# Spectral filter and feed-forward block: loads of x issued earlier in a period, and one first-stage piece of batch three one step sooner

## The chip, the cores and the metric

The kernel runs on one core of a Trainium2 chip. The metric is device time in microseconds; lower is better. A core has five engines that run side by side: TensorE (PE) multiplies matrices, VectorE (DVE) and ScalarE (ACT) work on elements, GpSimd (POOL) here only issues transfers, and SyncE (SP) only issues transfers too. Sixteen DMA engines move the data. Transfers issued by POOL run in one queue (q0) and those issued by SP in another (q1).

## The reference, cut to what matters

```python
# x: (8, 3008, 256), filters: (1505, 256)
X = np.fft.rfft(x, axis=1)
y = np.fft.irfft(X * (filt_r + 1j * filt_i)[None], n=3008, axis=1)
h = y.reshape(24064, 256) @ w_in            # (24064, 2048)
g = np.maximum(h, 0) + alpha * np.minimum(h, 0)
out = g @ w_out                             # (24064, 256)
```

## The kernel before, in words

**Two streams of work in one order.** The feed-forward part works on `yT`, the filtered sequence with the 256 features on partitions, in 48 blocks of 512 tokens (384 in blocks 5, 17, 29 and 41). A block has 16 steps, one for each 128 columns of `w_in`, so the program has 768 steps and block n begins at step 16n. In each step `up` (L473) issues two matmuls (L478) into a PSUM buffer `hps`; after every second step ScalarE evicts the pair to `gtb` (L486) and VectorE applies the slope (L489, L490). The second product, with `w_out`, is spread over the steps of the block after. Most blocks do it directly (`eight`, L515); the blocks of `FAST` do it with seven products in place of eight (`seven`, L537), for which sums of quarters of `gtb` are formed ahead (`sums`, L492): two on VectorE (L498, L500) and four as accumulating transfers that POOL issues, two of L502 (gtb<-gtb) and two of L504 (gtb<-ss). The table `SUMS` puts the latter at the steps 13, 17, 19 and 22 counted from the block's begin. The last of the seven products, sixteen matmuls, reads what L504 wrote: the first eight read the first transfer's half, the last eight the second's.

The filter is a Fourier transform done as matmuls, batch by batch, in stages that are put between these steps by hand. The function `put(step, fn)` files an action under a step, and the loop at the end calls, step by step, what is filed there and then `up`. An engine's queue, and SP's and POOL's queues of transfers, run in that order. For batch index b (0 to 7; batch three is b = 2) the stages are:

- **Load** (`load_x`, L145): the batch comes in four chunks `xs`, each in two transfers that POOL issues (L148), converting to 16 bits. There are four such buffers, so the chunks of a batch take the buffers of the batch before.
- **First stage** (`piece_a`, L182): 16 pieces, four to a chunk. One matmul (L190) into a PSUM bank `psF`, evicted by ScalarE to `asb` (L260). After each chunk `save_a` (L194, transfer at L195) writes `asb` to DRAM. There are two `asb` buffers, so chunk 3 (pieces 12 to 15) takes the buffer of chunk 1 (pieces 4 to 7).
- **Turn** (`turn_a`, L202): SP reads it back from DRAM into `at`, turned.
- **Second stage** (`piece_b`): 12 pieces, two matmuls each (L210), multiplied with the filter by VectorE into `ww` and `uu` (L213, L214), and joined by two accumulating transfers of POOL (L216, uu<-ww).
- **Third stage** (`piece_c`): two matmuls (L228), evicted to `v`. After every third piece `turn_c` (L231) writes part of `v` to DRAM in four transfers of SP (L237). After the last one three loads `zt` (L246) read it back; each waits until all writes have landed. The fourth `zt` load comes later.
- **Fourth stage** (`piece_d`): 16 pieces of four matmuls (L253) on `zt`, evicted to `yT`, where the feed-forward part reads.

All stage matmuls but some of the first batch's go through two `psF` banks, whose order is written out by hand in `BANKS`.

**Where the change lies.** For batches one and two (b = 1, 2) the steps come from `plan_fft` (L598). For b = 2 it has a0 = 66 and ga = 2, so piece i stands at step 66 + 2i: piece 7 at 80, and the save of its chunk at 80 too, after the second batch's last `turn_c` with its three `zt` loads, which is filed under step 80 first. Piece 12 stands at step 90, and the second batch's fourth stage begins at step 92. For b from 3 to 7 the steps count from p = 96(b − 1), the begin of a period of six blocks (p = 192, 288, 384, 480, 576), by the tables `STEPS_A` to `STEPS_D` (L29 to L32); its loads of the next batch are filed under p + 6, 10, 16 and 20 (L643), with b up to 6. The next batch's first pieces, which read these loads, stand at p + 15 and later. In a period the second stage stands at −19, −16, −16, −3, 1, 10 and later, the third at −5, 7, 8, 16, 20 and later. A block of `FAST` begins at each p, and another 32 steps ahead of p; the L504 transfers of that one are filed under p − 13 and p − 10.

Of the kernel before, what the change touches and what calls it, by code (L numbers as in the profile page):

```python
# [10 lines left out]
FP16 = mybir.dt.float16  # L11
# [6 lines left out]
D = 256  # L18
# [62 lines left out]
def kernel(  # L81
# [10 lines left out]
    nc = tc.nc  # L92
# [12 lines left out]
    p_as = ctx.enter_context(tc.tile_pool(name="p_as", bufs=2))  # L105
# [9 lines left out]
    a_dram = dram.tile([NB, 96, NH, D], FP16, name="a_dram")  # L115
# [25 lines left out]
    def xrow(b, h, c):  # L141
        return bass.AP(tensor=x.tensor, offset=x.offset + (b * NFFT + NH * h + 8 * c) * D,
                       ap=[[N2 * D, N1], [1, 8 * D]])

    def load_x(b, c):  # L145
        xs = p_x.tile([2 * N1, 8 * D], FP16, name="xs")
        for h in range(2):
            nc.gpsimd.dma_start(out=xs[h * N1 : h * N1 + N1], in_=xrow(b, h, c))  # L148
        return xs
# [14 lines left out]
    def bank(wide=False):  # L164
        if wide:
            return psH.tile([128, 2, 512], FP32, name="hps")[:, 0]
        return psF[int(next(order))].tile([128, 512], FP32, name="psF")
# [8 lines left out]
    class Fft:  # L176
        def __init__(self, b):
            self.b = b
            self.base = (b % 2) * NFFT
            self.uw, self.zt = {}, {}  # L180

        def piece_a(self, i, evict, wide=False):  # L182
            if i == 0:
                self.at = p_fft.tile([128, NK1, D], FP16, name="at")
            if i % 4 == 0:
                self.asb = p_as.tile([96, 8, D], FP16, name="asb")
            xs = xc[(self.b, i // 4)]
            ps = bank(wide)
            o = (i % 4) * 512
            nc.tensor.matmul(ps[0:96], wf1_s, xs[:, o : o + 512], start=True, stop=True)  # L190
            u = 2 * (i % 4)
            evict(self.asb[:, u : u + 2].rearrange("p a d -> p (a d)"), ps[0:96])

        def save_a(self, c):  # L194
            nc.sync.dma_start(out=a_dram[self.b, :, 8 * c : 8 * c + 8], in_=self.asb)  # L195

        def turn_a(self, eng, ka=0, kb=NK1):
            for h in range(2):
# [138 lines left out]
    xc = {(0, c): load_x(0, c) for c in range(4)}  # L337
# [76 lines left out]
    for q in range(2):  # L414
        nc.gpsimd.dma_start(
            out=wout_s[:, 8 * q : 8 * q + 8],
            in_=moe_w_out[1024 * q : 1024 * q + 1024].rearrange("(j p) d -> p j d", p=128))
# [177 lines left out]
    def put(step, fn, *args):  # L595
        plan.setdefault(step, []).append((fn, args))

    def plan_fft(b, a0, ga, ta, b0, gap, add, lag, d0, quarters, x_at):  # L598
        f = Fft(b)
        for i in range(16):  # L600
            put(int(a0 + ga * i), f.piece_a, i, on_act)
        for c in range(4):
            put(int(a0 + ga * (4 * c + 3)), f.save_a, c)
            if b + 1 < NB:
                put(x_at[c],
                    lambda b=b, c=c: xc.update({(b + 1, c): load_x(b + 1, c)}))
        for q in range(quarters):
            w = NK1 // quarters
            put(ta, f.turn_a, nc.sync, w * q, w * q + w)
        bs = [b0 + (2 * int(gap * kp / 2) if add else int(gap * kp)) for kp in range(12)]  # L610
        for kp in range(12):
            put(bs[kp], f.piece_b, kp)
            put(bs[kp] + lag, f.piece_c, kp, on_act)
        for q in range(4):
            put(bs[3 * q + 2] + lag + 1, f.turn_c, q)
        for i in range(16):
            put(d0 + min(i, 4) + 2 * max(i - 4, 0), f.piece_d, i, on_act)
        put(d0 + 5, f.load_z, 3)
# [9 lines left out]
    for i in range(4):  # L628
        put(26 + 3 * i, neg, 6 * i, 6 * i + 6)
    plan_fft(1, 16, 1, 32, 40, 3, 0, 6, 92, 4, (20, 24, 74, 75))  # L630
    plan_fft(2, 66, 2, 97, 109, 4.5, 8, 12, 187, 4, (110, 114, 118, 122))
    for b in range(3, NB):
        p = 96 * (b - 1)
        f = Fft(b)
        steps_a = STEPS_A if b > 3 else [int(2.4 * i) - 68 for i in range(16)]
        steps_b = STEPS_B if b > 3 else [max(st, 2 * kp - 12) for kp, st in enumerate(STEPS_B)]
        for i in range(16):
            put(p + steps_a[i], f.piece_a, i, on_act)
            if i % 4 == 3:
                put(p + steps_a[i] + 1, f.save_a, i // 4)  # L640
        if b + 1 < NB:
            for c in range(4):
                put(p + (6, 10, 16, 20)[c], lambda b=b, c=c: xc.update({(b + 1, c): load_x(b + 1, c)}))  # L643
        put(p + steps_a[15] + 4, f.turn_a, nc.sync)
        for kp in range(12):
            put(p + steps_b[kp], f.piece_b, kp)
            put(p + STEPS_C[kp], f.piece_c, kp, on_act)
            if kp % 3 == 2:
                put(p + STEPS_C[kp] + 1, f.turn_c, kp // 3)
        for i in range(16):  # L650
            put(p + STEPS_D[i], f.piece_d, i, on_act)
        put(p + STEPS_D[3] + 2, f.load_z, 3)
# [76 lines left out]
```

## Time and profile before

| what | value |
|---|---|
| median of three runs | 798.35 us (797.43 to 800.0) |
| the profiled execution | 798.93 us |
| its span, from the first to the last instruction | 797.1 us |
| granted TensorE clock, mean | 0.998 |
| instructions | 18089 |
| ScalarE busy / VectorE busy | 604.4 us / 685.0 us |
| transfers of POOL's queue (q0) | 50.09 MB, 38.6% of 16 DMA engines |
| transfers of SP's queue (q1) | 69.52 MB, 32.7% of 16 DMA engines |
| L148 loads of xs, 64 transfers, issue to landing | 6.6 us median |
| L502 and L504, 38 each, issue to landing | 4.5 and 6.4 us median |

The profile's page gives shares over the whole span. The waits view lists who waited for whom (total, number, longest). The timeline gives the instructions in order of time, merged where the same operation repeats; a bracket at the end is the engine's idle time before it and what ended it. Times count from the span's begin. Block 0 begins at 37.4 us, block 5 (step 80) at 125.0, block 11 (step 176) at 225.0, block 12 (step 192) at 243.0, block 30 (step 480) at 524.1.

### The profile page before, as it was taken

The numbers are of one execution on the slowest core, as the hardware profiler recorded it, in microseconds if no ns is written. First come the engines' busy times: TensorE is split into PE (matmuls) and PEld (weight loads), VectorE is DVE, ScalarE is ACT, GpSimd is POOL, SyncE is SP. The second block draws the span as 40 slices with busy tenths as digits, with TensorE's granted clock in tenths as the row PEclk, the third lists the DMA queues.
The fourth block names the chain that finished last, engine by engine and source line by source line (L and its number), as shares of the span: only waits on it lengthen the run. The fifth ranks groups of instructions, "written<-read, shape, count | busy, mean of one in ns | idle before, by whom it ended". The sixth has DMA issues, their size and how long they took to land.

```text
span 797.1 us, 18089 instructions
## 1 busy us (share of the span) xinstructions
PE 765.7 (96%) x6856; PEld 540.2 (68%) x6856; DVE 685.0 (86%) x1489; ACT 604.4 (76%) x896; POOL 266.5 (33%) x353
## 2 busy tenths in 40 slices
PE   7899998999999999999999999999999999999998
PEld 6756655666666766766667767667666777767766
DVE  3788984689778898999989999899998999979994
ACT  4688676877768887788868878688877777787763
POOL 7720441063223342452415422434423324102210
PEclk9999999999999999999999999999999999999999
DMA  9995557586596768986797956978688556645642
GB/s 191 186 210 159 110 123 197 142 146 138 119 204 123 151 148 179 205 161 144 168 194 157 189 136 153 237 144 164 142 182 199 108 97 121 154 86 104 129 95 67
DMA packets 113807, 120.84 MB, mean 152 GB/s; under 512 B 12648, under 2 KB 94328, under 8 KB 113592
## 3 DMA queue, kind: packets, MB, share of 16 engines
q0 software_dynamic: 33584, 50.09, 38.6%
q1 hardware_dynamic: 79992, 69.52, 32.7%
q8 instruction: 54, 0.88, 0.5%
q14 instruction: 33, 0.27, 0.1%
q10 hardware_dynamic: 144, 0.07, 0.0%
HBM read 56.06 MB, written 46.66 MB: 129 GB/s over the span
## 4 chain that ended last, share of the span: by engine, by line
PE 65%; DMA 13%; DVE 11%; ACT 6%; issue 3%; SPq 1%; POOL 1%; DVEq 0%; ACTq 0%; POOLq 0%
PE hps L478 28%; PE op L515 17%; PE op L537 9%; DVE m L489 4%; DMA gtb<-ss 4%; ACT gtb L486 3%; DMA at<-a_dram 3%; PE psF L190 3%; DVE gtb L490 3%; PE psF L228 2%; PE psF L253 2%; PE psF L210 2%; DMA uu<-ww 2%; DVE ww L213 1%; DVE uu L214 1%
## 5 line engine op out<-in xcount | busy, mean ns | idle before, releaser
L486 ACT ACTIVATE gtb<-hps 128x1024 f16<-128x1024 f32 (+1 forms) x384 | 385.7, 1005 | 109.9 <-PE hps L478 105.4
L478 PE MATMUL hps<-yT,win_s 128*128 128x512 f16 (+1 forms) x1536 | 450.0, 375 | 0.4 <-ACT gtb L486 0.2
L489 DVE TENSOR_SCALAR m<-gtb,alm_s 128x512 f16<-128x512 f16 (+1 forms) x768 | 235.6, 349 | 68.5 <-ACT gtb L486 65.9
L490 DVE TENSOR_TENSOR gtb<-gtb,m 128x1024 f16<-128x1024 f16 (+1 forms) x384 | 261.6, 681 | 18.4
L515 PE MATMUL op<-wout_s,gtb 128*128 128x256 f16 x1728 | 262.8, 273 | 0.0
L216 POOL DMA_DIRECT2D uu<-ww x168 | 140.2, 986 | 330.3 <-DVE uu L214 157.1
L515 PEld LDWEIGHTS <-gtb 128*128 128x128 f16 x1728 | 168.6, 98 | 114.1 <-issue 0.5
L478 PEld LDWEIGHTS <-win_s 128*128 128x128 f16 x1536 | 137.7, 98 | 32.1 <-issue 8.4
L537 PEld LDWEIGHTS <-gtb 128*128 128x128 f16 x1520 | 103.5, 97 | 49.2 <-DMA gtb<-ss 1.6
L502 POOL DMA_DIRECT2D gtb<-gtb x38 | 42.8, 1127 | 137.0 <-PE hps L478 43.5
L260 ACT ACTIVATE asb<-psF 96x512 f16<-96x512 f32 x112 | 66.1, 594 | 20.4 <-PE psF L190 16.8
L537 PE MATMUL op<-wout_s,gtb 128*128 128x128 f16 x912 | 77.5, 219 | 1.5 <-DMA gtb<-ss 0.8
L260 ACT ACTIVATE yT<-psF 128x376 f16<-128x376 f32 x120 | 56.7, 489 | 8.8 <-PE psF L253 7.7
L260 ACT ACTIVATE v<-psF 128x512 f16<-128x512 f32 x84 | 49.7, 598 | 16.4 <-PE psF L228 15.2
L213 DVE TENSOR_TENSOR ww<-psF,filts_s 128x512 f16<-128x512 f32 x84 | 57.4, 684 | 0.6 <-PE psF L210 0.6
L214 DVE TENSOR_TENSOR uu<-psF,filt_s 128x512 f16<-128x512 f32 x84 | 57.2, 681 | 0.0
L537 PEld LDWEIGHTS <-ss 128*128 128x128 f16 x608 | 42.6, 97 | 21.0
L537 PE MATMUL op<-tw_s,gtb 128*128 128x128 f16 x608 | 52.6, 219 | 0.0
L537 PE MATMUL op<-tw_s,ss 128*128 128x128 f16 x608 | 52.5, 219 | 0.0
L148 POOL DMA_DIRECT2D xs<-in_x_dram x64 | 44.3, 942 | 19.9 <-PE psF L190 13.0
L190 PE MATMUL psF<-xs,wf_s 94*96 94x512 f16 x112 | 42.2, 383 | 5.6 <-ACT asb L260 3.4
L504 POOL DMA_DIRECT2D gtb<-ss x38 | 41.5, 1236 | 6.6 <-PE hps L478 2.6
(85 smaller groups left out, 506.0 us busy)
## 6 DMA issues: line engine op xcount, KB each, us to landing
out_dram<-osb SPq DMA_DIRECT2D x127, 128.0 KB
xs<-in_x_dram POOLq DMA_DIRECT2D x64, 188.0 KB, 6.6
a_dram<-asb SPq DMA_DIRECT2D x28, 384.0 KB
uu<-ww POOLq DMA_DIRECT2D x168, 64.0 KB, 3.1
v_dram<-v SPq DMA_DIRECT2D x112, 96.0 KB
zt<-v_dram SPq DMA_DIRECT2D x28, 384.0 KB
gtb<-gtb POOLq DMA_DIRECT2D x38, 256.0 KB, 4.5
gtb<-ss POOLq DMA_DIRECT2D x38, 256.0 KB, 6.4
```

The costliest lines, as they stand in the source:

```text
L148: nc.gpsimd.dma_start(out=xs[h * N1 : h * N1 + N1], in_=xrow(b, h, c))
L190: nc.tensor.matmul(ps[0:96], wf1_s, xs[:, o : o + 512], start=True, stop=True)
L213: nc.vector.tensor_mul(ww, px, filts_s[:, 2 * kp : 2 * kp + 2])
L214: nc.vector.tensor_mul(uu, px, filt_s[:, 2 * kp : 2 * kp + 2])
L216: nc.gpsimd.dma_start(out=uu[o : o + 64], in_=ww[64 - o : 128 - o], accum_op=OP.add)
L260: nc.scalar.activation(o, i, AF.Copy)
L478: nc.tensor.matmul(self.hps[:, j % 2, 0:tn], win_s[:, kt, j * 128 : (j + 1) * 128], yT[:, kt, self.t0 : self.t0 + tn], start=(kt == 0), st ...
L486: nc.scalar.activation(g, hs, AF.Copy)
L489: nc.vector.tensor_scalar(ms[:, i], g[:, i], 0.0, a, OP.min, OP.mult)
L490: nc.vector.tensor_add(g, g, ms)
L515: nc.tensor.matmul(op[:, si % 2], self.pair(k // 2)[:, k % 2, 128 * si : 128 * si + 128], wout_s[:, k], start=(k == 0), stop=(k == 15))
L537: nc.tensor.matmul(acc[:, 128 * i : 128 * i + 128], x[:, k, 128 * i : 128 * i + 128], b[:, k], start=first and k + i == 0, stop=k == 7, sk ...
```

## The change

One: for b = 3 to 6 the loads of the next batch's four chunks are filed under p − 8, p − 4, p and p + 4 in place of p + 6, p + 10, p + 16 and p + 20. Two: for b = 2, piece 7 and the save of its chunk are filed under step 79 in place of 80. Three: the `asb` buffers are kept by chunk, in a dictionary, in place of one name for the latest.

```diff
         def __init__(self, b):
             self.b = b
             self.base = (b % 2) * NFFT
-            self.uw, self.zt = {}, {}
+            self.uw, self.zt, self.asb = {}, {}, {}
...
             if i % 4 == 0:
-                self.asb = p_as.tile([96, 8, D], FP16, name="asb")
+                self.asb[i // 4] = p_as.tile([96, 8, D], FP16, name="asb")
...
-            evict(self.asb[:, u : u + 2].rearrange("p a d -> p (a d)"), ps[0:96])
+            evict(self.asb[i // 4][:, u : u + 2].rearrange("p a d -> p (a d)"), ps[0:96])
...
-            nc.sync.dma_start(out=a_dram[self.b, :, 8 * c : 8 * c + 8], in_=self.asb)
+            nc.sync.dma_start(out=a_dram[self.b, :, 8 * c : 8 * c + 8], in_=self.asb[c])
...
         for i in range(16):
-            put(int(a0 + ga * i), f.piece_a, i, on_act)
+            put(int(a0 + ga * i) - (b == 2 and i == 7), f.piece_a, i, on_act)
         for c in range(4):
-            put(int(a0 + ga * (4 * c + 3)), f.save_a, c)
+            put(int(a0 + ga * (4 * c + 3)) - (b == 2 and c == 1), f.save_a, c)
...
             for c in range(4):
-                put(p + (6, 10, 16, 20)[c], lambda b=b, c=c: xc.update({(b + 1, c): load_x(b + 1, c)}))
+                put(p - 8 + 4 * c, lambda b=b, c=c: xc.update({(b + 1, c): load_x(b + 1, c)}))
```

The instruction lists show what moves. VectorE's order is the same. On TensorE one L190 moves ahead of the two L478 and four L515 of step 79. On ScalarE one eviction to `asb` moves ahead of one eviction to `gtb`. On SP one save (L195) moves ahead of four v writes (L237) and three zt loads (L246). On POOL, in the periods with p = 288, 384 and 480, the order L504 twice, L216 four times, L148 four times, L216 twice, L502, L148 twice, L502, L504, L148 twice, L504 becomes L504 twice, L148 four times, L216 twice, L148 twice, L216 twice, L148 twice, L216 twice, L502 twice, L504 twice.

## The prediction

> **What bounds the kernel now.** I read the page first: how full TensorE is, and whether one place or many hold its idle time.
>
> ```profile
> span 797.1 us, 18089 instructions
> PE 765.7 (96%) x6856; PEld 540.2 (68%) x6856; DVE 685.0 (86%) x1489; ACT 604.4 (76%) x896; POOL 266.5 (33%) x353
> ```
>
> TensorE is busy for 765.7 of 797.1 us, so a change to transfers can win only where TensorE is seen waiting. The waits view names one long wait in the middle of the run:
>
> ```profile
> ACT asb L260 <- DMA a_dram<-asb: 3.6, 1, 3.6
> PE psF L190 <- ACT asb L260: 3.4, 2, 3.0
> ```
>
> ScalarE waited once, 3.6 us, for a save of asb to land, and TensorE waited 3.0 us of the 3.4 for that ScalarE instruction. The timelines of SP's queue, ScalarE and TensorE place it. Columns: start, length, engine, line, tiles, count, idle before.
>
> ```profile
> 124.75 2.77 SPq L237 DMA_DIRECT2D v_dram<-v  x4
> 130.38 1.25 SPq L246 DMA_DIRECT2D zt<-v_dram  x3
> 131.72 0.38 SPq L195 DMA_DIRECT2D a_dram<-asb  x1
> 145.68 0.31 SPq L195 DMA_DIRECT2D a_dram<-asb  x1
> 148.99 1.29 SPq L202 DMA_DIRECT2D at<-a_dram  x3
> ```
>
> ```profile
> 124.12 0.60 ACT L260 ACTIVATE v<-psF 128x512 f16<-128x512 f32 x1 [0.24 <-PE psF L228]
> 124.62 1.02 ACT L486 ACTIVATE gtb<-hps 128x1024 f16<-128x1024 f32 x1
> 125.52 0.59 ACT L260 ACTIVATE asb<-psF 96x512 f16<-96x512 f32 x1
> 137.89 0.59 ACT L260 ACTIVATE asb<-psF 96x512 f16<-96x512 f32 x1 [3.65 <-DMA a_dram<-asb]
> ```
>
> ```profile
> 135.25 0.33 PE L253 MATMUL psF<-wi_s,zt 96*128 96x94 f16 x4
> 138.53 0.38 PE L190 MATMUL psF<-xs,wf_s 94*96 94x512 f16 x1 [2.95 <-ACT asb L260]
> ```
>
> The third batch's second chunk was evicted to asb at 125.52 and its save was ready from 126.1. SP's queue runs in order: the save stood behind the second batch's three zt loads, which wait until the v writes have landed, and went out at 131.72. There are two asb buffers, so the eviction of the fourth chunk's first piece stood from 134.2 to 137.89. The L190 behind it needed the psF bank that this eviction was to empty, so TensorE stood idle for 2.95 us before 138.53. Then its clock fell. The windows view (length, busy time and count of five engines, clock, DMA share, GB/s) shows it, with another window after a shorter gap:
>
> ```profile
> 139.28:142.69 3.41, 3.41 (x21) 2.21 (x20) 1.87 (x6) 2.66 (x6) 0.00 (x0) 0.50 0.09 29
> 237.20:241.00 3.80, 3.79 (x35) 2.82 (x36) 2.50 (x6) 2.89 (x5) 1.66 (x2) 1.00 0.46 78
> ```
>
> ```profile
> 237.21 0.39 PE L228 MATMUL psF<-uu,twi_s 128*128 128x256 f16 x2 [1.71 <-DMA uu<-ww]
> ```
>
> For 3.41 us the granted clock was 0.50: half of it, 1.7 us, was lost, of which I take 1.65 since the ends fall within instructions. After the idle 1.71 us at 237.21 it stayed 1.00. The one stall thus costs 2.95 + 1.65 = 4.60 us.
>
> **The change part by part.**
>
> *Piece 7 of batch three and its save, from step 80 to 79.* Nothing is added. On SP the save now stands before the four v writes and three zt loads. On TensorE one L190 goes ahead of step 79's matmuls; it needs the psF bank of piece 6, whose eviction is the one before the v eviction and ended by 124.12 − 0.24 = 123.88, about when the L190 would start: no new wait, at most a tenth of a us. On ScalarE one asb eviction goes ahead of one gtb eviction, which starts about 0.5 us later (125.12 for 124.62) and is made up by the next one: hidden. The save goes out near 125.3 instead of 131.72. A save with little beside it landed 3.3 us after its issue (145.68, whose reader was released at 148.99), so even twice that ends at 131.9, before the eviction wants the buffer at 134.2. The 4.60 us go.
>
> What is late next is zt. The first v write waited for the v eviction, whose row ends at 124.72; now it waits for the asb eviction (0.58 later) and a save's issue (0.38): 0.96 us. If the save's 384 KB also took DMA time from the v writes, at 295 GB/s (the row of 132 to 134) it adds up to 1.3. Its room is seen in two windows:
>
> ```profile
> 130.00:132.00 2.00, 2.00 (x17) 1.41 (x16) 1.20 (x4) 1.55 (x3) 0.00 (x0) 1.00 0.24 55
> 132.00:134.00 2.00, 2.00 (x16) 1.46 (x15) 1.11 (x3) 1.87 (x4) 0.00 (x0) 1.00 0.99 295
> ```
>
> The DMA engines are a quarter busy from 130 to 132, so most of it fits there: I put the zt issue at 131.4 (between 131.3 and 132.7). Its first load lands after 3.3 us (the lone save) to 4.8 (issued at 130.38, read at 135.25 without a wait). TensorE reads at 135.25: the wait is 0 to 2.2 us. I take 0.3, from a landing after 4.1 us.
>
> *Loads of x for batches five to eight, from steps 6, 10, 16, 20 of a period to −8, −4, 0, 4.* The same 32 transfers on POOL's queue. Their buffers are free (last read at step −32 or −37) and they are first wanted at step 15 of the period, so their own time is covered. What matters is which transfers they stand beside. They wait for no engine, so POOL issues them as soon as the instruction before them is out:
>
> ```profile
> 514.97 3.16 POOL L504 DMA_DIRECT2D gtb<-ss  x2
> 524.71 1.67 POOL L216 DMA_DIRECT2D uu<-ww  x2 [6.58 <-DVE osb L457]
> 528.43 2.71 POOL L148 DMA_DIRECT2D xs<-in_x_dram  x4
> 538.15 1.51 POOL L502 DMA_DIRECT2D gtb<-gtb  x1
> 538.73 2.02 POOL L148 DMA_DIRECT2D xs<-in_x_dram  x2
> ```
>
> This is the period whose step 0 is at 524.06. Now four x transfers follow the L504 pair directly, near 517 to 520; the uu transfers at 524.71 and after come behind them, and are read some 14 us later (the third-stage pieces of steps 16 and 20), which covers the x loads ahead of them. The L502 and L504 of steps 13 to 22 lose the x loads among them. There TensorE waited a little, twice:
>
> ```profile
> 366.02 0.80 PE L537 MATMUL op<-wout_s,gtb 128*128 128x128 f16 x7
> 552.67 0.76 PE L537 MATMUL op<-wout_s,gtb 128*128 128x128 f16 x7
> 524.49 0.55 PE L537 MATMUL op<-wout_s,gtb 128*128 128x128 f16 x7
> ```
>
> Seven such matmuls take 0.55; these took 0.80 and 0.76, so 0.25 + 0.21, say 0.44 us, can be won. The price is at the L504 pair that now has x behind it. Its last landing against its reader, by issue plus landing, in the three periods that have such a pair (the source view of L504):
>
> ```profile
> L504 POOL DMA_DIRECT2D gtb<-ss x2: 1923/2054/2185, 328.7 to 330.0; - x2
> DMA to landing us min/median/max: 7.1/7.1/7.1
> ...
> L504 POOL DMA_DIRECT2D gtb<-ss x2: 1924/2046/2167, 515.0 to 516.2; - x2
> ...
> DMA to landing us min/median/max: 7.6/7.6/7.6
> ```
>
> ```profile
> 336.84 0.56 PE L537 MATMUL op<-wout_s,gtb 128*128 128x128 f16 x7
> 523.82 0.23 PE L537 MATMUL op<-wout_s,gtb 128*128 128x128 f16 x1 [0.30 <-DMA gtb<-ss]
> ```
>
> 330.0 + 7.1 = 337.1, its reader (the seventh at 336.84) starts at 337.18: 0.1 us to spare. 516.2 + 7.6 = 523.8, where TensorE already waits: none. The period between has about 0.3. A delay d in each costs (d − 0.1) + (d − 0.3) + d = 3d − 0.4. For d there is the first L502 of a block, with x loads issued right behind it (at 444.8 and 538.2) and without (at 475.0 and 567.5); in this order the source view of L502 in a window around each gives:
>
> ```profile
> DMA to landing us min/median/max: 3.9/3.9/3.9
> DMA to landing us min/median/max: 5.5/5.5/5.5
> DMA to landing us min/median/max: 4.5/4.5/4.5
> DMA to landing us min/median/max: 3.9/3.9/3.9
> ```
>
> With x behind, mean 4.7; without, mean 4.2: d = 0.5, between 0 (a later transfer cannot hasten an earlier one) and 1.6. Cost 1.1 us; at the upper end 4.4.
>
> The Trainium skill, "DMA: Bandwidth & Descriptors", section "Queues, rings and completion order", says that the descriptors of one ring are consumed in order. By that rule d is 0 and the time would be 793.6; the 5.5 beside 3.9 speaks against it in part, as the start in order need not keep the ends apart.
>
> **Sum.** −2.95 − 1.65 + 0.3 + 1.1 − 0.44 = −3.64 us. The profiled execution took 798.93 (span 797.1 and 1.83 around it), so 795.29; it stands 0.58 above the median 798.35, so I predict **794.7**. The times below have the 0.58 taken off too.
>
> **Rivals.**
> 1. *The wait moves to zt.* At the upper end 2.2 in place of 0.3: 796.6; 798.3 if the clock falls as well. For it: zt was on time by at most 1.6 us (135.25 − 130.38 − 3.3). Against: the DMA share of 0.24 just before.
> 2. *Slower: x delays the L504 pairs.* If the DMA engines shared their time between a pair and the x loads behind it, rather than finishing the pair first, each pair would land up to four x transfers late. Four x loads issued together landed 1.1 us apart,
>
> ```profile
> L148 POOL DMA_DIRECT2D xs<-in_x_dram x4: 1033/1038/1148, 435.4 to 437.1; - x4
> DMA to landing us min/median/max: 4.7/5.7/6.4
> ```
>
> first at 435.4 + 4.7, last at 437.1 + 6.4, so 3.4 for three and 4.5 for four. Cost 3 × 4.5 − 0.4 = 13.1, and 806.7 in all. It outweighs the rest from d = 1.7 us. Against: x behind an L502 never cost over 1.6.
> 3. *The x part does nothing.* TensorE waits for no x load now; without gain or price there, −4.30: 794.1.
> 4. *The clock falls anyway.* Then the 1.65 stays: 796.4. Against: the fall began 0.75 us after the stall, and the 1.71 us gap caused none. The Trainium skill, "TensorE: Matmul & The Clock Gate", Part 1, has the clock halve after an idle window of about 3.4 us; by that rule 2.95 us would be too short and this rival right, but the 0.50 beside the stall says otherwise.
>
> **How the numbers follow.** Forecast 0.60, rival 1 0.12, rival 2 0.10, rival 3 0.13, rival 4 0.05. About 0.3% (2.4 us) is what a measurement of this kernel can tell from no change, so faster means below 795.95: most of the forecast, rival 3 and half of rival 1, 0.76. Slower is most of rival 2, 0.08; the rest, 0.16, is within. Low end: no cost of zt or d, −5.04 and so 793.3, less 0.5 as the median of a few runs can lie lower (the runs before reached from 797.43 to 800.0): 792.8. High end: d = 1.6 gives 798.0, above zt at its worst (796.6) and rival 4 (796.4): 798.0. Outside lie rival 2 and the tails, some 0.13.
>
> **What would show it.** The wait of ScalarE for a_dram<-asb gone and no window of clock 0.50 before the end; the save issued near 125.3, before the v writes; the first L253 on the second batch's zt with under 0.5 us idle; xs right after the L504 pair; the last L537 before each of those three periods 0.5 us later, the rows of seven near 366 and 552 back to 0.55. A zt wait over 3 us, or L537 waits over 1.8 us each, make it wrong.

## The result, and the profile after

| | before | after |
|---|---|---|
| median of seven runs on one chip, us | 799.37 (797.43 to 802.16) | 794.86 (793.37 to 795.84) |
| span of the profiled execution, us | 797.1 | 793.1 |

The ratio is 0.9935 [0.9915, 0.9956]: a gain of two thirds of a percent, clear of the spread. The page of the profile after shows the same work in a shorter span:

```profile
span 793.1 us, 18081 instructions
PE 763.7 (96%) x6856; PEld 539.9 (68%) x6856; DVE 685.0 (86%) x1489; ACT 604.3 (76%) x896; POOL 265.8 (34%) x353
```

TensorE is busy for 2.0 us less with the same 6856 matmuls; 1.7 of them are the stretch of clock 0.50, which is gone. The timelines of SP's queue, ScalarE and TensorE after, around block 5:

```profile
127.53 0.31 SPq L195 DMA_DIRECT2D a_dram<-asb  x1
127.89 3.71 SPq L237 DMA_DIRECT2D v_dram<-v  x4
133.85 1.26 SPq L246 DMA_DIRECT2D zt<-v_dram  x3
```

```profile
126.92 0.58 ACT L260 ACTIVATE asb<-psF 96x512 f16<-96x512 f32 x1
136.44 0.59 ACT L260 ACTIVATE asb<-psF 96x512 f16<-96x512 f32 x1
```

```profile
127.33 0.49 PE L478 MATMUL hps<-yT,win_s 128*128 128x384 f16 x2
...
137.56 0.33 PE L253 MATMUL psF<-wi_s,zt 96*128 96x94 f16 x4
137.73 0.38 PE L190 MATMUL psF<-xs,wf_s 94*96 94x512 f16 x1
...
142.12 0.60 PE L478 MATMUL hps<-yT,win_s 128*128 128x512 f16 x2
```

The first and the last of TensorE's rows are the begins of blocks 5 and 6. The same two in the timeline before:

```profile
125.01 0.49 PE L478 MATMUL hps<-yT,win_s 128*128 128x384 f16 x2
...
144.56 0.60 PE L478 MATMUL hps<-yT,win_s 128*128 128x512 f16 x2
```

Block 5 took 144.56 − 125.01 = 19.55 us and takes 142.12 − 127.33 = 14.79: 4.76 us gained, against 2.95 + 1.65 = 4.60 in the sum. The eviction at 136.44 and the L190 at 137.73 have no bracket: nothing waits. In the windows view the clock is 1.00 where it was 0.50:

```profile
137.00:142.00 5.00, 5.00 (x53) 3.93 (x52) 2.92 (x8) 4.57 (x10) 0.00 (x0) 1.00 0.91 292
```

Block 5 begins 2.32 us later than before because this one execution has a wait in block 1, where the two kernels issue the same instructions (ScalarE's waits from 50 to 70 us, and TensorE's row behind it):

```profile
ACT asb L260 <- DMA a_dram<-asb: 2.0, 1, 2.0
```

```profile
62.39 0.38 PE L190 MATMUL psF<-xs,wf_s 94*96 94x512 f16 x1 [2.09 <-ACT asb L260]
```

The begin of each block after less its begin before, by their first L478, shows where the span's difference arises: +0.2 us at block 0, +2.2 at block 2 (the wait of block 1), +2.3 at block 5, −2.4 at block 6, −2.9 at block 12, −3.1 at block 20, −3.5 at block 35, −4.1 at block 47, the last. Block 5 makes the gain, some 1.7 us more come in small steps behind it, and in this execution block 1 takes 2 us back. Most of the small steps are of this one pair of executions: in the kernel after taken again (e9, below) the difference is −4.1 at block 6 and −3.9 at block 47.

### The profile page after: what moved, and what is told of

Same layout as the page of the kernel before. It is cut to its first block, busy times and chain, and to the rows that moved or that the text cites. A ratio compares the mean times of both kernels' runs of the same rounds, so it can differ in the third digit from the quotient of the medians.

```text
span 793.1 us, 18081 instructions
## 1 busy us (share of the span) xinstructions
PE 763.7 (96%) x6856; PEld 539.9 (68%) x6856; DVE 685.0 (86%) x1489; ACT 604.3 (76%) x896; POOL 265.8 (34%) x353
## 4 chain that ended last, share of the span: by engine, by line
PE 68%; DMA 11%; DVE 9%; ACT 6%; issue 3%; SPq 1%; POOL 1%; DVEq 0%; ACTq 0%; POOLq 0%
PE hps L478 30%; PE op L515 18%; PE op L537 9%; DVE m L489 3%; PE psF L190 3%; DMA at<-a_dram 3%; ACT gtb L486 3%; DMA gtb<-ss 2%; PE psF L228 2%; DMA uu<-ww 2%; DVE gtb L490 2%; PE psF L210 2%; PE psF L253 2%; DMA twf_s<-c_twf 1%; DMA a_dram<-asb 1%
## 5 line engine op out<-in xcount | busy, mean ns | idle before, releaser
L478 PE MATMUL hps<-yT,win_s 128*128 128x512 f16 (+1 forms) x1536 | 449.2, 374 | 0.4 <-ACT gtb L486 0.2
L515 PE MATMUL op<-wout_s,gtb 128*128 128x256 f16 x1728 | 262.0, 272 | 0.0
L216 POOL DMA_DIRECT2D uu<-ww x168 | 140.7, 989 | 316.6 <-DVE uu L214 158.7
L515 PEld LDWEIGHTS <-gtb 128*128 128x128 f16 x1728 | 168.5, 98 | 113.5
L478 PEld LDWEIGHTS <-win_s 128*128 128x128 f16 x1536 | 137.7, 98 | 30.7 <-issue 7.0
L537 PEld LDWEIGHTS <-gtb 128*128 128x128 f16 x1520 | 103.5, 98 | 48.8 <-DVE gtb L490 1.1
L502 POOL DMA_DIRECT2D gtb<-gtb x38 | 43.3, 1139 | 142.5 <-DVE ss L498 43.9
L537 PE MATMUL op<-wout_s,gtb 128*128 128x128 f16 x912 | 77.3, 219 | 1.3 <-DMA gtb<-ss 0.7
L537 PEld LDWEIGHTS <-ss 128*128 128x128 f16 x608 | 42.6, 98 | 21.0
L148 POOL DMA_DIRECT2D xs<-in_x_dram x64 | 45.9, 1000 | 20.6 <-PE psF L190 12.9
L537 PE MATMUL op<-tw_s,gtb 128*128 128x128 f16 x608 | 52.5, 219 | 0.0
L537 PE MATMUL op<-tw_s,ss 128*128 128x128 f16 x608 | 52.5, 219 | 0.0
L190 PE MATMUL psF<-xs,wf_s 94*96 94x512 f16 x112 | 42.0, 380 | 4.7 <-ACT asb L260 2.6
L504 POOL DMA_DIRECT2D gtb<-ss x38 | 40.5, 1210 | 10.2 <-PE op L537 5.5
```

The source lines that it names most:

```text
L216: nc.gpsimd.dma_start(out=uu[o : o + 64], in_=ww[64 - o : 128 - o], accum_op=OP.add)
L478: nc.tensor.matmul(self.hps[:, j % 2, 0:tn], win_s[:, kt, j * 128 : (j + 1) * 128], yT[:, kt, self.t0 : self.t0 + tn], start=(kt == 0), st ...
L515: nc.tensor.matmul(op[:, si % 2], self.pair(k // 2)[:, k % 2, 128 * si : 128 * si + 128], wout_s[:, k], start=(k == 0), stop=(k == 15))
L537: nc.tensor.matmul(acc[:, 128 * i : 128 * i + 128], x[:, k, 128 * i : 128 * i + 128], b[:, k], start=first and k + i == 0, stop=k == 7, sk ...
```

## The experiments

Two theories stood against each other. By theory **A** the whole gain comes from the piece and its save: the chunk's buffer is free sooner, the stall and the fall of the clock go, and the loads of x do next to nothing. By theory **B** the loads of x have their own part, a gain at the rows of seven L537 and a price at the L504 pairs behind which they now stand. Each kernel was compared with the kernel before on the same chip; three chips were used, and its medians there were 799.31, 798.66 and 798.52.

### Part one alone: e1_piece

```diff
# against before: self.asb by chunk as in the change, and
-            put(int(a0 + ga * i), f.piece_a, i, on_act)
+            put(int(a0 + ga * i) - (b == 2 and i == 7), f.piece_a, i, on_act)
-            put(int(a0 + ga * (4 * c + 3)), f.save_a, c)
+            put(int(a0 + ga * (4 * c + 3)) - (b == 2 and c == 1), f.save_a, c)
```

> Part one alone: piece 7 of batch three and its save at step 79, loads of x where they were. Theory (the saved stall and clock drop are the whole gain): 4.6 us off the time before, ratio near 0.9943; no wait of ScalarE for a_dram<-asb in block 5, clock 1.00 there, block 5 at 14.8 us as after the change; the L537 rows of seven near steps 334 and 527 still 0.76 to 0.80 us. Rival (the x loads carry a share): under 3 us off, ratio above 0.9963.

Measured: 795.41 us, ratio 0.9948 [0.9934, 0.9963], span 792.7. Block 5 takes 15.30, half a us more than after, since here the zt loads land a little late. The zt loads in SP's queue and their first reader:

```profile
131.03 1.25 SPq L246 DMA_DIRECT2D zt<-v_dram  x3
```

```profile
135.03 0.34 PE L253 MATMUL psF<-wi_s,zt 96*128 96x94 f16 x4 [0.33 <-DMA zt<-v_dram]
```

The piece alone gives the gain within the interval of the whole change. The rows of seven L537 lie in blocks 19 and 31. These take 15.14 us each here, with the loads of x in their old place, as they do after (before: 15.39 and 15.35), so e1 lacks the excess that was expected there. It has one in block 13 in its place, 15.63 us against 15.20 before and after; point 4 below counts this kind of wait over all runs.

### Part two alone: e2_loads

```diff
# against before
-                put(p + (6, 10, 16, 20)[c], lambda b=b, c=c: xc.update({(b + 1, c): load_x(b + 1, c)}))
+                put(p - 8 + 4 * c, lambda b=b, c=c: xc.update({(b + 1, c): load_x(b + 1, c)}))
```

> Part two alone: loads of x at steps -8 to 4, piece 7 at step 80. Theory: 0.2 us off or nothing (0.44 won at two L537 rows, 0.25 paid at the three L504 pairs), ratio 0.999 to 1.001; block 5 keeps its 2.95 us wait and the clock of 0.50. Rival (the x loads carry a share): 1.5 us or more off, ratio under 0.998.

Measured: 799.47 us, ratio 1.0011 [0.9986, 1.0037]: no difference. The stall stays, and in this execution a second place crosses the line at which the clock falls. TensorE's rows, and the two windows behind them:

```profile
138.87 0.38 PE L190 MATMUL psF<-xs,wf_s 94*96 94x512 f16 x1 [2.80 <-ACT asb L260]
...
237.79 0.39 PE L228 MATMUL psF<-uu,twi_s 128*128 128x256 f16 x2 [1.96 <-DMA uu<-ww]
```

```profile
139.57:142.97 3.40, 3.40 (x21) 2.16 (x19) 1.81 (x6) 2.60 (x6) 0.00 (x0) 0.50 0.11 36
238.55:241.96 3.41, 3.41 (x21) 2.25 (x20) 1.31 (x3) 1.87 (x4) 2.24 (x4) 0.50 0.94 154
```

The wait at 237.79 is that of 237.21 before, 0.25 us longer. That isn't the moved loads' doing: after has them in the same place and waits 1.31 us there, e1 hasn't and waits 1.46. In the measured time e1 and e2 together are theory A. A part of the loads as small as half a us, which the profiles do show (points 4 and 5 below), is beyond what these intervals can tell.

### Another buffer in place of the earlier save: e3_spare

The queue's order stays that of before; the chunk gets room of its own in a part of `tw_s` that is idle then, so its slow save holds no one up.

```diff
# against before: self.asb by chunk, and
+SPARE = ((2, 1),)
-                self.asb[i // 4] = p_as.tile([96, 8, D], FP16, name="asb")
+                if (self.b, i // 4) in SPARE:
+                    o = 2048 * SPARE.index((self.b, i // 4))
+                    self.asb[i // 4] = tw_s.rearrange("p a k c -> p (a k c)")[0:96, o : o + 2048].rearrange("p (s d) -> p s d", d=D)
+                else:
+                    self.asb[i // 4] = p_as.tile([96, 8, D], FP16, name="asb")
```

> The kernel before, with chunk 1 of batch three in a buffer of its own (a part of tw_s that is idle then), so that nothing waits for its save; the order of all queues is that of before. Theory (the wait for the buffer is the whole cost, not the place of the zt loads): the same 4.6 us off, ratio near 0.9943, clock 1.00 in block 5. Rival (something else in block 5, such as the zt loads or the DMA load, would hold TensorE next): a new wait of 1 us or more there, ratio above 0.9965.

Measured: 796.36 us, ratio 0.9957 [0.9944, 0.997], span 794.6; block 5 takes 14.79. SP's queue (lines stand 5 further down here):

```profile
124.71 2.48 SPq L242 DMA_DIRECT2D v_dram<-v  x4
129.75 1.25 SPq L251 DMA_DIRECT2D zt<-v_dram  x3
131.09 0.38 SPq L200 DMA_DIRECT2D a_dram<-tw_s  x1
```

The save still leaves after the zt loads, at 131.09, and the stall is gone all the same. So it was the buffer that TensorE waited for in the end, not the data, as the prediction's chain had it.

### A spare buffer for the wait in block 1: e4_after_spare

```diff
# against after: as e3, for another chunk
+SPARE = ((1, 2),)
```

> The changed kernel, with chunk 2 of batch two in a buffer of its own, so that its evictions in block 1 don't wait for the save of chunk 0. The profile of the changed kernel has a wait of 2.0 us there that the profile of before lacks, in a stretch where both run the same instructions. Theory (that wait is of the single run: the DMA engines are full there, and the save lands sooner or later): 0 to 2 us off the changed kernel's time depending on the run, 4.6 to 6.6 us off the time before, and less spread between runs; block 1 at 20.8 us or less. Rival (the change made that wait): always 2 us off the changed kernel's time.

Measured: 795.48 us, ratio 0.9943 [0.9927, 0.996]; the whole change has 0.9935 [0.9915, 0.9956], so nothing is won that the intervals show. The wait in block 1 comes and goes in one and the same kernel: the profile of after has it, and that of after taken again (e9) doesn't. Of the others e8 has it, 1.6 us, e2 has 0.7 us at the same row, and before, e1, e3, e5, e6 and e7 have at most 0.5.

### The stall made smaller in two steps: e5_p12_1 and e5_p12_2

The eviction that waits is that of piece 12. Filed one or two steps later, it asks for the buffer later, and TensorE idles for less.

```diff
# against before; the second kernel has 2 * (b == 2 and i == 12)
-            put(int(a0 + ga * i), f.piece_a, i, on_act)
+            put(int(a0 + ga * i) + (b == 2 and i == 12), f.piece_a, i, on_act)
```

> The kernel before, with piece 12 of batch three one step later (91 for 90), so that the same wait for the buffer begins 0.9 us later: TensorE's idle time in block 5 about 2.1 us in place of 2.95. Theory (the clock falls when enough of a stretch of 3.41 us is idle, as 2.95 and, in the run with the loads alone, 1.96 us were): it falls still, a window of 3.41 us at 0.50, block 5 at about 18.7 us. Rival (it takes an idle stretch of nearly 3 us, or the fall has another cause): clock 1.00 throughout block 5 and 17.0 us, or, with another cause, a fall at the same place whatever the idle time.

> The same, two steps later (92): idle time about 1.2 us, a third of a stretch of 3.41. Theory: the clock stays at 1.00, and block 5 takes 14.8 + 1.2 = 16.0 us; stall and clock drop go together. Rival (the fall has another cause): a window of 0.50 in block 5 again.

Measured, one execution each: 802.22 and 796.65 us. One step later, TensorE's row and the window behind it:

```profile
138.83 0.59 PE L190 MATMUL psF<-xs,wf_s 94*96 94x512 f16 x1 [2.19 <-ACT asb L260]
```

```profile
138.56:141.96 3.40, 3.13 (x15) 1.87 (x15) 1.11 (x3) 2.32 (x6) 0.00 (x0) 0.50 0.34 124
```

Two steps later:

```profile
138.25 0.33 PE L253 MATMUL psF<-wi_s,zt 96*128 96x94 f16 x4 [1.59 <-ACT asb L260]
```

```profile
138.20:141.60 3.40, 3.35 (x36) 2.62 (x36) 1.11 (x3) 3.35 (x7) 0.00 (x0) 1.00 0.27 99
```

After 2.19 us idle the clock falls, after 1.59 (and 0.45 more at a second, smaller wait) it doesn't. Block 5 takes 18.65 and 17.15, the second 1.1 us more than was expected, with 1.59 and 0.45 us idle in place of 1.2. Against the 14.79 without a stall the first loses 3.86 us, the idle 2.19 and half of the 3.4 us window; so stall and clock are two terms that can be taken away one by one, as the sum had them. The total of the first is no measure of this: its profile has two further falls, at 22.5 and 333.1 us, far from the edit.

### The loads of x ahead of the L504 pair: e6_ahead

The change files the loads behind the pair. Here four x transfers stand ahead of it, in the three periods that have such a pair.

```diff
# against after
-                put(p - 8 + 4 * c, lambda b=b, c=c: xc.update({(b + 1, c): load_x(b + 1, c)}))
+                put(p - 14 if b > 3 and c < 2 else p - 8 + 4 * c, lambda b=b, c=c: xc.update({(b + 1, c): load_x(b + 1, c)}))
```

> The changed kernel, with the first two chunks of x of batches six to eight filed at step -14, so that four x transfers stand ahead of the L504 pair in POOL's queue and not behind it. Theory (transfers of one queue are finished nearly in order, so x behind costs 0.1 us and x ahead costs its own time): the pair lands 4 to 4.5 us later in three periods, TensorE waits about 4 us for gtb<-ss at each, with a fall of the clock there; span 12 to 17 us longer than the changed kernel's 793.1. Rival (the DMA engines share their time between what is queued): little difference to the changed kernel, under 3 us.

Measured in one execution: 815.27 us, span 813.4, which is 20.3 longer than after and more than the 12 to 17 that were expected. TensorE's waits, POOL's queue in the last of the three periods, TensorE's row there and the windows behind the three waits:

```profile
PE op L537 <- DMA gtb<-ss: 13.6, 4, 4.4
```

```profile
524.52 3.37 POOL L148 DMA_DIRECT2D xs<-in_x_dram  x4
527.75 1.93 POOL L504 DMA_DIRECT2D gtb<-ss  x2
```

```profile
536.96 0.39 PE L537 MATMUL op<-wout_s,gtb 128*128 128x128 f16 x2 [4.00 <-DMA gtb<-ss]
```

```profile
338.10:341.50 3.40, 3.40 (x25) 2.52 (x26) 1.11 (x3) 1.29 (x2) 0.00 (x0) 0.50 0.77 167
437.10:440.50 3.40, 3.40 (x24) 2.45 (x23) 1.31 (x3) 1.51 (x2) 0.00 (x0) 0.50 0.97 196
536.10:542.90 6.80, 5.94 (x36) 4.12 (x37) 2.40 (x5) 2.22 (x3) 0.15 (x1) 0.50 0.68 136
```

13.6 us of waiting, against 0.7 after, and half of 3.4 + 3.4 + 6.8 us at clock 0.50: 12.9 + 6.8 = 19.7 of the 20.3. The three pairs have 4.45, 4.13 and 4.00 us of the waiting, and the last fall of the clock lasts twice as long as the others. This is the price that the prediction's slower rival feared (4.5 us for each pair), and it is real; but it is paid by what stands behind the x loads in the queue. What stands ahead of them pays next to nothing (point 5 below).

### The wait that is left: e7_b3 and e8_c0

After the change the longest wait inside the run is in block 11, 1.3 us for the uu transfers of batch three (TensorE's row after):

```profile
234.35 0.39 PE L228 MATMUL psF<-uu,twi_s 128*128 128x256 f16 x2 [1.31 <-DMA uu<-ww]
```

Two ways to remove it: file the piece that feeds them two steps sooner (e7), or the piece that reads them five steps later (e8).

```diff
# e7, against after
-        steps_b = STEPS_B if b > 3 else [max(st, 2 * kp - 12) for kp, st in enumerate(STEPS_B)]
+        steps_b = STEPS_B if b > 3 else [max(st, 2 * kp - 12 - 2 * (kp == 0)) for kp, st in enumerate(STEPS_B)]
# e8, against after (the second line keeps every piece's bank as it was)
+BANKS = BANKS[:163] + "10101101011" + BANKS[174:]
-            put(p + STEPS_C[kp], f.piece_c, kp, on_act)
+            put(p + STEPS_C[kp] + 5 * (b == 3 and kp == 0), f.piece_c, kp, on_act)
```

> The changed kernel, with the first second-stage piece of batch four (b = 3) two steps sooner (-14 for -12), so that its uu transfers are issued 1.7 us before. Theory (the next such stall, 1.3 to 2.0 us for uu<-ww in block 11 in every profile so far, and now and then a fall of the clock with it, goes the same way): 1.3 to 1.8 us off the changed kernel, 6 to 7 us off the time before, ratio 0.991 to 0.9925; block 11 at 16.2 us. Rival (at<-a_dram is not there yet at step -14, or the uu transfers land no sooner): a wait of the same size at L210 or L228 in block 11, ratio as the changed kernel's, 0.9935.

> The changed kernel, with the first third-stage piece of batch four (b = 3) five steps later (0 for -5), so that TensorE asks for its uu transfers 5 us later and not that they are issued sooner; eleven entries of the bank order are rewritten to fit. Theory (these transfers land when the burst of zt loads and stores in SP's queue is through, whenever they are issued; the stall is of the reader's place): the wait for uu<-ww in block 11 goes, block 11 at 16.4 us for 17.6, 1.3 us or a little less off the changed kernel, ratio 0.991 to 0.9925 to before. Rival (the wait moves to the next reader, a piece of the fourth stage or a bank): ratio as the changed kernel's, 0.993 to 0.994.

Measured: e7 794.21 us, ratio 0.9936 [0.9914, 0.9959]; e8 793.09, ratio 0.9926 [0.9896, 0.9956]. In e7 the wait is still there, as its rival had it. TensorE's row, the source view of L216 and a window in which the transfers run:

```profile
231.96 0.39 PE L228 MATMUL psF<-uu,twi_s 128*128 128x256 f16 x2 [1.28 <-DMA uu<-ww]
```

```profile
L216 POOL DMA_DIRECT2D uu<-ww x2: 814/973/1132, 225.8 to 226.3; - x2
DMA to landing us min/median/max: 5.6/5.7/5.7
```

```profile
228.00:230.00 2.00, 2.00 (x15) 1.32 (x14) 1.97 (x5) 1.56 (x3) 0.47 (x1) 1.00 1.06 263
```

The same pair after the change, by the source view of the same line and the windows of its transfers:

```profile
L216 POOL DMA_DIRECT2D uu<-ww x2: 814/973/1132, 229.9 to 230.5; - x2
DMA to landing us min/median/max: 3.8/4.0/4.2
```

```profile
230.00:232.00 2.00, 2.00 (x16) 1.37 (x14) 2.00 (x4) 1.56 (x3) 1.59 (x2) 1.00 1.03 260
232.00:234.40 2.40, 1.09 (x12) 0.73 (x10) 2.37 (x6) 1.11 (x2) 2.01 (x4) 1.00 0.80 149
```

Block 11 begins at 220.13 in e7 and at 222.50 after. The first of the pair is issued 5.7 us after that begin in e7 and 7.4 after it in after, 1.7 us sooner; the second lands 226.3 + 5.6 − 220.13 = 11.8 and 230.5 + 3.8 − 222.50 = 11.8 us after it. All of the 1.7 us is lost in the transfer. In e7 it runs wholly beside SP's loads and stores, at a DMA share of 1.0; after, it runs at their end, where the share is 1.03 and then 0.80. That these make it late is likely and not shown. In e8 the reader moved instead, and block 11 goes from 17.59 us (after; 17.58 in e7) to 16.63: no L228 waits there any more, and 0.45 us of waiting is left at an L254. On the same chip e8's median stands 1.3 us below that of after (next), within intervals that overlap.

### After, once more: e9_after

The kernel after without an edit, beside e8 on the same chip, for the spread and for the wait in block 1.

> The changed kernel once more, beside the run before it on the same chip: ratio to before 0.9935 with an interval of 0.2%. Theory of the single wait in block 1 (of the run, not of the change): block 1 at 20.8 us this time, span near 791 to 792. Rival: 22.8 us again.

Measured: 794.42 us, ratio 0.994 [0.9915, 0.9965], span 793.3. No such wait in block 1, which takes 20.84 us (22.82 after), and block 5 at 14.79 again. The span is still over the 791 to 792 that were expected: in this execution the clock fell once in the start-up, at 21.67 us, well before the first block.

## Why the prediction was right, point by point

Forecast 794.7 us, measured 794.86; its sum held in its large terms and in the gain of the loads, and missed in their price. That the two times agree to 0.2 us is in part luck, as the end of this section says.

1. **The stall goes, −2.95 and −1.65.** Right, and shown: −4.76 us in block 5. e1 has it without the loads, e2 has the loads without it, e3 has it by another buffer, and e5 takes idle time and clock apart.
2. **The save near 125.3, zt issued at 131.4.** Block 5 begins 2.32 us later after than before, so the save at 127.53 is 125.2 and the zt issue at 133.85 is 131.5 in the clock of before: right.
3. **A new wait on zt, 0.3 in a range of 0 to 2.2.** The first L253 starts without a bracket after, 0.33 late in e1, 0.70 in e7. Block 5 takes 14.79 us in five of the seven runs with the save moved, 0.51 more in e1 and 0.88 more in e7: 0.2 in the mean. The size is right and below what one execution tells from the next. Rival 1, 2.2 us there, is out.
4. **The two rows of seven L537, −0.44.** Right as a gain of the moved loads, though not bound to these two rows. The four periods whose loads move begin with blocks 12, 18, 24 and 30, and the seven products of these run in the blocks after them: 13, 19, 25 and 31. Added up, these four take 60.73 us in every one of the seven profiles with the loads moved. In the five with the loads in their old place they take 61.19 (before), 61.16 (e1), 61.74 (e3), 61.64 and 61.63 (e5): 0.43 to 1.01 more, 0.74 in the mean. The excess of block 19 stands in before alone, that of block 31 in before, e3 and both of e5, that of block 13 in e1. In e5 (two steps) TensorE's row in block 31 names its cause, and the row that took 0.76 before takes 0.55 after:

```profile
551.55 0.23 PE L537 MATMUL op<-wout_s,gtb 128*128 128x128 f16 x1 [0.72 <-DMA gtb<-ss]
```

```profile
549.62 0.55 PE L537 MATMUL op<-wout_s,gtb 128*128 128x128 f16 x7
```

   The two L504 transfers that block 31 reads, by the source view before and after:

```profile
L504 POOL DMA_DIRECT2D gtb<-ss x2: 894/996/1099, 542.2 to 544.3; - x2
DMA to landing us min/median/max: 7.8/8.3/8.9
...
L504 POOL DMA_DIRECT2D gtb<-ss x2: 856/882/907, 539.1 to 541.1; - x2
DMA to landing us min/median/max: 4.5/4.6/4.6
```

   With the loads of x out of the way the pair lands 3.2 to 4.3 us sooner. This holds in every run: the second of the two lands after 8.6 to 9.7 us in the five profiles and after 4.6 to 4.7 in the seven. Most of that is spare time, so the gain is small and differs from run to run.

5. **The price at the L504 pairs, +1.1 from a delay d of 0.5.** Mis-sized. The pair in the source view after, in the third of the three periods:

```profile
L504 POOL DMA_DIRECT2D gtb<-ss x2: 1922/2043/2164, 511.8 to 513.1; - x2
DMA to landing us min/median/max: 7.6/7.6/7.7
```

   Landing of the second transfer of each pair, mean of the three periods: with the x loads elsewhere 7.35 (before), 7.76 (e1), 7.60 (e3), 7.47 and 7.56 (e5), together 7.55 us; with x right behind 7.53 (after), 7.53 (e2), 7.97 (e4), 7.72 (e7), 7.71 (e8), 7.71 (e9), together 7.70. So d is 0.15, within the spread of single runs, and costs 0.05 + 0 + 0.15 = 0.2 by the prediction's own terms. The 0.5 compared the first L502 of different blocks. The same one in blocks 18, 24 and 30 takes 4.7, 3.9 and 5.5 us with x right behind it (mean of the five profiles) and 4.4, 4.3 and 4.8 without (mean of seven): a difference of 0.3, −0.4 and 0.7, 0.2 in the mean. So most of the 0.5 lay between the blocks. The Trainium skill, "DMA: Bandwidth & Descriptors", section "Queues, rings and completion order", has one ring's descriptors consumed in order; a d this small beside the 4.0 to 4.5 us of e6 agrees with it, and the weight that the prediction gave to the 5.5 against it was wrong.
6. **POOL's order.** As read from the instruction lists. In the timeline of POOL after, x stands right behind the pair:

```profile
325.81 3.15 POOL L504 DMA_DIRECT2D gtb<-ss  x2
327.58 3.46 POOL L148 DMA_DIRECT2D xs<-in_x_dram  x4
```

By the profiles the moved loads win 0.74 us in the mean (point 4) and cost some 0.2 (point 5). No median here can tell the difference from nothing: e2 has 1.0011 [0.9986, 1.0037], and e1 0.9948 beside 0.9935 and 0.994 for the whole change. Rival 3, the x part does nothing, is near in size and wrong in mechanism. Rival 4, the clock falls without the stall, is out: 1.00 in block 5 of after, e1 and e3.

With the terms as the runs have them (−4.60, 0.2 for zt, 0.2 for the pairs, and the −0.44 as it was) the sum is −4.6, near the −4.51 between the medians of before and after. The forecast's −3.64 was about a us too small, nearly all of it by d. The forecast time came out right all the same because it counted from 798.35, the median of three runs, where the median of seven is 799.37: that 1.0 us is luck. The medians of before on the other chips, 799.31, 798.66 and 798.52, show how much such a start can vary.

## What to carry to other kernels

When an eviction waits for its buffer, look at which queue the buffer's save stands in and what it stands behind: a save that is ready but queued behind loads that wait for something else can hold TensorE, and one step in the queue, or a buffer more, is worth the stall and the clock behind it. Independent loads cost next to nothing behind an urgent pair of the same queue (0.15 us here) and some 4 us ahead of it, so read the queue's order, not only the time of issue. A wait of a few tenths of a us, seen in one execution, should be looked for in others, and in the sister blocks too: here one of the two excesses came back in three of four other profiles and larger, the other in none.

## What the runs showed of the hardware that was not expected

**The clock falls after less idle time than one of its stretches.** It fell after TensorE's idle times of 2.95 (before), 2.80 and 1.96 (e2), 2.19 (e5, one step) and 4.0 to 4.45 us (e6), and did not after 1.71 (before), 1.59 (e5, two steps) and 2.09 (after, block 1, where the window of 3.4 us behind it has clock 1.00). So the length alone doesn't decide: 1.96 fell and 2.09 didn't. Falls in one run lie whole multiples of 3.41 us apart: 238.55 − 139.57 = 98.98 = 29.0 × 3.413 in e2, and 338.1, 437.1, 536.1 in e6, again 29.0 each. On such a grid the stretch before the second fall of e2, 235.14 to 238.55, holds its idle time whole, 1.96 of 3.41 or 57%. The record of the granted clock in the trace of after fixes its grid too: the first rise to 1.00 is at 6.53 us and the last fall at 795.01, just behind the span's end, 231.0 stretches apart, so an edge lies at 61.14, within the wait of 2.09 us (60.30 to 62.39). That leaves 0.84 us of it in one stretch and 1.25, or 37%, in the next.

Such a grid can be laid over each of the twelve traces by its own record. Of the whole stretches between the first rise and the end of the span, the clock fell behind every one with 1.89 us of idle time or more in sum (1.89 is e9's, before 21.67) and behind none with 1.69 or less. Between them, at 1.71 to 1.76 us, it fell once (e5, one step, at 333.12) and stayed three times (before, after and e4). So the fall takes about half a stretch of idle time. The Trainium skill, "TensorE: Matmul & The Clock Gate", Part 1, has the window run freely, at about 3.4 us, with which the grid agrees; where it asks for an idle window the runs differ: one idle for 55% was enough.

**A transfer issued sooner, into another queue's burst, landed no sooner.** In e7, 1.7 us at the issue were 0 at the landing, as the transfer took 5.6 to 5.7 us in place of 3.8 to 4.2. The Trainium skill, "DMA: Bandwidth & Descriptors", section "Queues, rings and completion order", has a DMA engine take turns between its queues packet by packet. The longer time amid SP's stores fits that, but no run here sets it apart from other causes.
